# Attention with two feed-forwards: the second output product as seven products, and a new opening

## The chip, the core and the metric

The kernel runs on one core of one Trainium2 chip. The metric is the device time of one execution in microseconds. Before the change the median of three runs was 813.78 us (812.83 to 814.72). Every time below comes from these runs or from one profiled execution.

## The reference

Attention over 4 batches, 8 heads, 576 positions and 64 numbers a head (heads 0 to 3 see the last 32 positions, heads 4 to 7 every 32nd), then a gated feed-forward, then a second one whose hidden layer is the largest of three products. All tensors are float32.

```python
scores = np.where(masks, scale * np.matmul(q, k.transpose(0, 1, 3, 2)), -1e9)
attn = softmax(scores)                                # heads 0-3 local, 4-7 strided
x = np.matmul(attn, v).transpose(0, 2, 1, 3).reshape(2304, 512)
g = x @ w_gate                                        # 512 x 1536
x = (g * sigmoid(g) * (x @ w_val)) @ w_out            # 1536 x 512
h = np.maximum(np.maximum(x @ w1, x @ w2), x @ w3)    # 512 x 768 each
return h @ w_out2                                     # 768 x 512
```

## The kernel before

**Precision.** Every factor of a matmul is held as a high part in fp32r (a shorter float) and a low part, the difference. A product is three matmuls: high by high, high by low, low by high (`product`, `split`).

**First stage.** The rows of x are handled in five chunks of 512 or 448 tokens. Attention runs in blocks of two rows of 32 tokens for all heads; what it yields is split and kept as `xh`, `xl`. For each chunk and each of 12 blocks f of the hidden layer, the gate product (`ps_g`), the value product (`ps_v`) and the output product (`ps_y`) follow one another. In chunk 0 the raw 64-bit weights are loaded and rounded to float32 as well (`raw`; steps `size`, `rounding`, `sign`, `clamp`, `shift`, `rounded`), split, and stored for the later chunks.

The opening and chunk 0 run in the order of a table, `FIRST`, in which a letter is a step and a number the block or the weight: l and m load an attention block's queries, keys and values; S is its scores (L387), M, E, R the softmax, N its last step on POOL, T the transposes (L427), V their copy out of the banks, P the products with the values (L458), H and L the split into `xh` (L468) and `xl` (L474). r loads a raw weight, a, q, s, c, t, d round it, h and o split it, y stores it. G0 is the first half of the first gate product, b0 its second half, B and O are value and output products. The program order is the order of each engine's instructions there. `ON_SCALAR` lists the weights whose sign is taken on ScalarE (L209), with a cheaper shift on VectorE (L223); for the others POOL takes it (L211), with the dearer shift L225. All DMAs here are issued by SyncE, in program order.

**Between.** Chunks 1 to 4 are ordered by a scheduler. Steps named `later` convert the second stage's weights beside them: `pair_steps` makes, for w1, w2, w3 and each of three groups g of two blocks of h, the seven pieces of a Strassen-like product (seven half-size products in place of eight), `wo2_steps` splits the output weight of one block.

**Second stage.** Three passes p of 768 tokens, in two halves of 384 columns. In a pass there are nine `Group`s, g = 0 to 2 and i = 0 to 2 for w1 to w3. A group has `head`, `middle` and `tail` with 42 matmuls of 128x384 (L775): weight pieces (A11, A12, S3, A22, S1, S2, S4) come from a ring of four tiles of 1792 KB (`load_w`), the factors of y (B11, B21, T2, T1, T3, T4, B22) are made by sums and split once per pass (`load_y`, `split_y`, L173 and L176). A group's tail comes behind the next one's head. Copies of a bank to SBUF (`snap`, L789) and sums lead to four blocks of h; the last i takes the maximum, and its result is split per block. Then the output product follows: for each of six blocks j of 128 tokens, six blocks f of h stand in TensorE as weights and `wo2` (3072 KB, loaded once) streams through, 512 columns a time, 108 matmuls per pass (L849, banks `ps_z`). The first two j begin before the last tail with blocks f 0 to 3 (`z_early`). The y of the next pass is loaded during the first groups of this one.

## Time and profile before

| | us |
|---|---|
| median of three runs | 813.78 (812.83 to 814.72) |
| the profiled execution | 814.75 |
| its span | 813.0 |
| TensorE busy | 795.3 (98% of the span) |
| TensorE loading weights | 711.5 (88%) |
| VectorE busy | 542.8 (67%) |
| ScalarE busy | 384.2 (47%) |
| POOL busy | 235.6 (29%) |

The mean granted clock is 0.996. Busy times of matmuls overlap, since they are pipelined, so that 98% says that TensorE is seldom idle and not that it runs at its peak. The first stage ends near 530 us and the second begins there. In a row of a line or a tile, an arrow reads from right to left: the output's name stands left, the inputs' names right, and x counts instructions.

### The profile page before, as it was taken

The page shows a single profiled execution, that of the slowest core. Times are in us where ns is not written, and L with a number is a line of the kernel's source. Part 1 is how long each engine was busy: PE and PEld are TensorE (multiplying, and loading weights), DVE is VectorE, ACT ScalarE, POOL GpSimd, SP SyncE. Part 2 cuts the span into 40 slices and gives each one's busy share as a digit, 9 for nine tenths or more (in the row PEclk, how much of TensorE's full clock was granted, in tenths as well). Part 3 has the DMA queues.
Part 4 walks back from the last instruction along what each step waited for, and adds up shares of the span by engine and source line. Part 5 has one row for each costly group of instructions (what it writes and reads, how often), then busy time and mean ns, then how long its engine had stood idle before and what let it go on. Part 6 is the DMA issues. An engine that isn't in the chain of part 4 may idle for free.

```text
span 813.0 us, 12942 instructions
## 1 busy us (share of the span) xinstructions
PE 795.3 (98%) x4588; PEld 711.5 (88%) x4588; DVE 542.8 (67%) x1104; ACT 384.2 (47%) x856; POOL 235.6 (29%) x237
## 2 busy tenths in 40 slices
PE   6999999999999999999999999999999999999998
PEld 5777777888998998888999999999999989989986
DVE  5899997888969899799993863634454344613440
ACT  6999994455454634555342543423242123512220
POOL 2534442022312432314232664502212121402110
PEclk9899999999999999999999999999999999999999
DMA  9998887777766887757676997789646566634402
GB/s 281 322 326 290 303 311 270 262 242 226 261 235 208 264 285 246 264 208 258 231 262 212 346 392 294 281 342 354 237 181 232 168 210 213 260 148 181 181 1 77
DMA packets 69688, 200.50 MB, mean 247 GB/s; under 512 B 8088, under 2 KB 33432, under 8 KB 66040
## 3 DMA queue, kind: packets, MB, share of 16 engines
q1 hardware_dynamic: 69480, 199.55, 70.0%
q8 instruction: 36, 0.59, 0.3%
q14 instruction: 28, 0.23, 0.1%
q10 hardware_dynamic: 144, 0.13, 0.0%
HBM read 157.97 MB, written 41.68 MB: 246 GB/s over the span
## 4 chain that ended last, share of the span: by engine, by line
PE 55%; DVE 4%; DMA 2%; issue 1%; ACT 1%; SPq 0%; POOL 0%; DVEq 0%; ACTq 0%
PE ps_a L775 13%; PE ps_z L849 9%; PE ps_c L775 7%; PE ps_b L775 3%; PE ps_y L645 3%; PE ps_y L647 3%; PE ps_y L646 3%; PE ps_v L645 3%; PE ps_v L647 3%; PE ps_v L646 2%; PE ps_g L645 2%; PE ps_g L646 2%; PE ps_g L647 2%; DMA wr<-wsdr 1%; DVE pr L552 1%
## 5 line engine op out<-in xcount | busy, mean ns | idle before, releaser
L680 POOL TENSOR_TENSOR hl<-ht,hh 128x448 fp32r<-128x448 f32 x48 | 61.6, 1284 | 228.1 <-ACT hh L676 206.4
L176 POOL TENSOR_TENSOR hl<-t,hh 128x384 fp32r<-128x384 f32 x36 | 37.7, 1050 | 208.0 <-ACT hh L173 160.0
L775 PE MATMUL ps_a<-yhT,wr 128*128 128x384 f32 x324 | 94.6, 339 | 1.1 <-ACT s L789 1.1
L645 PE MATMUL ps_g<-xh,wh_g 128*128 128x448 f32 (+1 forms) x240 | 90.8, 378 | 1.0 <-ACT ht L664 1.0
L645 PE MATMUL ps_v<-xh,w_v 128*128 128x448 f32 (+1 forms) x240 | 91.2, 380 | 0.4 <-DVE ht L671 0.2
L646 PE MATMUL ps_g<-xl,wh_g 128*128 128x448 f32 (+1 forms) x240 | 89.8, 374 | 0.0
L647 PE MATMUL ps_y<-hh,w_o 128*128 128x448 f32 (+1 forms) x240 | 89.4, 373 | 0.3 <-DVE w_o L249 0.3
L647 PE MATMUL ps_g<-xh,wl_g 128*128 128x448 f32 (+1 forms) x240 | 89.5, 373 | 0.0
L646 PE MATMUL ps_y<-hl,w_o 128*128 128x448 f32 (+1 forms) x240 | 89.2, 372 | 0.0
L646 PE MATMUL ps_v<-xl,w_v 128*128 128x448 f32 (+1 forms) x240 | 89.2, 372 | 0.0
L647 PE MATMUL ps_v<-xh,w_v 128*128 128x448 f32 (+1 forms) x240 | 89.1, 371 | 0.0
L789 ACT ACTIVATE s<-ps_a 128x384 f32<-128x384 f32 x81 | 39.4, 490 | 99.0 <-PE ps_a L775 98.7
L676 ACT ACTIVATE hh<-ht 128x448 fp32r<-128x448 f32 (+1 forms) x60 | 35.3, 588 | 104.7 <-DVE ht L671 93.4
L645 PE MATMUL ps_y<-hh,w_o 128*128 128x448 f32 (+1 forms) x240 | 84.3, 380 | 0.0
L849 PE MATMUL ps_z<-wo2t,hh 128*128 128x512 f32 x216 | 64.8, 392 | 0.9 <-ACT osb L867 0.7
L775 PEld LDWEIGHTS ps_a<-yhT,wr 128*128 128x128 f32 x324 | 59.7, 188 | 2.6 <-ACT s L789 2.1
L775 PE MATMUL ps_a<-ylT,wr 128*128 128x384 f32 x162 | 54.8, 338 | 0.0
L645 PEld LDWEIGHTS ps_g<-xh,wh_g 128*128 128x128 f32 x240 | 45.4, 189 | 7.1 <-ACT ht L664 1.8
L645 PEld LDWEIGHTS ps_v<-xh,w_v 128*128 128x128 f32 x240 | 45.1, 188 | 6.5 <-DVE ht L671 1.1
L647 PEld LDWEIGHTS ps_g<-xh,wl_g 128*128 128x128 f32 x240 | 45.3, 189 | 5.4 <-DVE wl_g L249 0.4
L647 PEld LDWEIGHTS ps_y<-hh,w_o 128*128 128x128 f32 x240 | 45.1, 188 | 5.6 <-DVE w_o L249 0.7
L645 PEld LDWEIGHTS ps_y<-hh,w_o 128*128 128x128 f32 x240 | 45.0, 188 | 5.6
(150 smaller groups left out, 1843.2 us busy)
## 6 DMA issues: line engine op xcount, KB each, us to landing
wr<-wsdr SPq DMA_DIRECT2D x27, 1792.0 KB, 7.3
raw<-in_w_dram SPq DMA_DIRECT2D x60, 512.0 KB, 6.0
w_v<-wvdr SPq DMA_DIRECT2D x48, 512.0 KB, 4.5
w_o<-wodr SPq DMA_DIRECT2D x48, 512.0 KB, 4.6
wsdr<-whi SPq DMA_DIRECT2D x27, 256.0 KB, 2.9
wvdr<-w_v SPq DMA_DIRECT2D x12, 512.0 KB, 3.7
wodr<-w_o SPq DMA_DIRECT2D x12, 512.0 KB, 3.9
wsdr<-w SPq DMA_DIRECT2D x18, 256.0 KB, 3.3
```

The source lines that it names most:

```text
L176: return a.ins, lo_eng.tensor_tensor(lo, src, f32(hi), ALU.subtract).ins
L552: eng.tensor_tensor(pv, self.k[:, 0:i + 1, :], self.q[:, r:r + 1, :].to_broadcast([128, i + 1, D]), ALU.mult)
L645: nc.tensor.matmul(ps, wh, xh, start=first, stop=False)
L646: nc.tensor.matmul(ps, wh, xl, start=False, stop=False)
L647: nc.tensor.matmul(ps, wl, xh, start=False, stop=last)
L676: return nc.scalar.activation(hs[c, f][0], t, AF.Copy).ins
L680: return eng.tensor_tensor(hl, t, f32(hh), ALU.subtract).ins
L775: nc.tensor.matmul(ps, wts[:, c, a, ks], y[k][b], start=first and k == q == 0, stop=k == 1 and q == 2, skip_group_check=True,)
L789: nc.scalar.activation(s, self.a, AF.Copy)
L849: nc.tensor.matmul(z[j], a[:, ts], w[:, f, b], start=f == q == 0, stop=f == NF2 - 1 and q == 2)
```

## The change

The output product of the second feed-forward takes the seven-product form too, and it is turned: pieces of w_out stand as weights, h streams with 384 columns, and the output is stored transposed (the host turns it). `pair_steps` makes the pieces of w_out (i = 3) in place of `wo2_steps`, and they come through the ring, which has five tiles now: 36 loads of 1792 KB, where there were 27 and one of 3072. A pass has 126 matmuls of 128x384 for it (`Out`, `outputs`), the parts with g = 0 and 1 of three pieces before and behind the last group's tail. h is no longer split per block; its seven factors are made and split per group (`Factors`). What is to be converted waits in a list (`waiting`), from which `some(n)` takes entries at chosen places. The y of the next pass is loaded at the end of a pass, into single buffers. The second stage and the last two blocks of the last chunk run in program order, without the scheduler.

The table `FIRST` is new: the first raw weight's load stands behind the sixth block's (l5, m5), the transposes, copies and products of the blocks stand in another order, and so do the steps of chunk 0. Five more weights take their sign on ScalarE, the copies of blocks 3, 6 and 7 and the high part of block 3 go to VectorE.

```diff
@@ -53,34 +53,34 @@
-l0 k0 l1 l2 l3 l4 m4 k1 r0 l5 m5 l6 m6 l7 m7 r1 r2 r3 r4 S0 M0 S1 E0 M1 S2 E1 R0 M2 S3 N0 T0 E2 M3 S4 R1
...
+l0 k0 l1 l2 l3 l4 m4 k1 l5 m5 r0 l6 m6 l7 m7 r1 r2 r3 r4 S0 M0 S1 E0 M1 S2 R0 E1 N0 M2 S3 E2 R1 T0 M3 N1
+S4 V0 E3 R2 T1 P0 N2 M4 V1 T2 R3 P1 E4 V2 N3 H0 S5 L0 T3 H1 M5 P2 V3 E5 L1 P3 R4 N4 H3 a0 S6 R5 q0 c0 L3
...
-ON_SCALAR = range(5, 3 * NF, 2)
-
-NRING = 4
+ON_SCALAR = (0, 3, 4, 5, 7, 9, 10, 11, 13, 15, 17, 18, 19, 21, 23, 25, 27, 29, 31, 33, 35)
+
+NRING = 5
...
+    OUT_PIECES = ("A11", "S3", "A12", "A22", "S1", "S2", "S4")
...
+            if i == 3:
+                a12, a21 = a21, a12
...
-    def wo2_steps(f):
...
+        eng = nc.vector if (c, f) == (NC - 1, NF - 1) else nc.gpsimd
+        last_val[:] = [m, high_h(c, f, t), low_h(c, f, t, eng)]
...
+    class Factors:
...
+        def combine(self):
+            b12 = self.raw["T3"]
+            nc.vector.tensor_tensor(self.fresh("T1"), b12, self.raw["B11"], ALU.subtract)
+            nc.gpsimd.tensor_tensor(b12, self.raw["B22"], b12, ALU.subtract)
+            nc.vector.tensor_tensor(self.fresh("T2"), self.raw["B22"], self.raw["T1"], ALU.subtract)
+            nc.vector.tensor_tensor(self.fresh("T4"), self.raw["B21"], self.raw["T2"], ALU.subtract)
+
+        def split(self, f):
+            src = self.raw.pop(f)
+            hi, lo = self.part("h", f), self.parts.get(f) or self.part("l", f)
+            self.parts[f] = hi, lo
+            split(hi, lo, src, nc.scalar, nc.gpsimd if f in ("T3", "B22") else nc.vector)
+
+    waiting = []
+
+    def some(n):
+        for _ in range(min(n, len(waiting))):
+            waiting.pop(0)()
+
+    def conversion(fs, names):
+        return [fs.combine] + [lambda f=f: fs.split(f) for f in names]
+
+    def load_y(p):
+        y = [Factors(y_p, f"y{k}") for k in range(2)]
...
+        for k in range(2):
+            waiting.extend(conversion(y[k], FACTORS[:-1]))
+        waiting.extend(lambda k=k: y[k].split("B22") for k in range(2))
...
+            t = to = run[blk]
+            if self.i == 2:
+                h2.setdefault(self.g, Factors(h2_p, f"h{self.g}"))
+                to = h2[self.g].fresh("T3") if blk == "12" else t
+                h2[self.g].raw.setdefault("B" + blk, t)
             if s is None:
-                nc.vector.tensor_tensor(t, ps, t, ALU.max)
+                nc.vector.tensor_tensor(to, ps, t, ALU.max)
             else:
                 nc.vector.tensor_tensor(s, ps, s, ALU.add)
-                nc.vector.tensor_tensor(t, s, t, ALU.max)
-            if self.i == 2:
-                f, h = 2 * self.g + int(blk[0]) - 1, int(blk[1]) - 1
-                hh, hl = h2[f]
-                ts = slice(h * TB, (h + 1) * TB)
-                split(hh[:, ts], hl[:, ts], t, nc.scalar, nc.gpsimd)
+                nc.vector.tensor_tensor(to, s, t, ALU.max)
 
...
+        def finish(self):
+            if self.i == 2:
+                waiting.extend(conversion(h2[self.g], FACTORS))
...
-    def mm(j, fs):
-        if True:
-            if j not in z:
-                z[j] = z_p.tile([128, 512], F32, name="ps_z", tag="z")
-            ts = slice(j * 128, (j + 1) * 128)
-            for f in fs:
-                (hh, hl), w = h2[f], wo2
-                for q, (a, b) in enumerate(((hh, 0), (hh, 1), (hl, 0))):
-                    nc.tensor.matmul(
-                        z[j], a[:, ts], w[:, f, b], start=f == q == 0, stop=f == NF2 - 1 and q == 2
-                    )
-
-    def out2(p):
...
+    class Out:
...
+        def mul(self, n, piece, f, gs=range(NFP), last=False):
+            ms = slice(self.m * 128, (self.m + 1) * 128)
+            factor_product(
+                getattr(self, n), OUT_PIECES, piece, [(self.w[g], ms) for g in gs], [h2[g].parts[f] for g in gs],
+                gs[0] == 0 and piece in ("A11", "A12", "S1"), last
+            )
+
...
+        def emit(self, blk, ps, s=None):
+            t0 = (2 * PASSES[self.p] + int(blk[1]) - 1) * TB
+            rows = slice((int(blk[0]) - 1) * 256 + self.m * 128, (int(blk[0]) - 1) * 256 + (self.m + 1) * 128)
+            osb = osb_p.tile([128, TB], F32, name="osb", tag="osb")
+            if s is None:
+                nc.scalar.activation(osb, ps, AF.Copy)
             else:
-                nc.scalar.activation(osb, z[j], AF.Copy)
-            nc.sync.dma_start(out[t0:t0 + 128, :], osb)
-
-        for j in range(2 * TB // 128):
-            mm(j, z_late if j < 2 else range(NF2))
-            done(j)
-        z.clear()
-
+                nc.vector.tensor_tensor(osb, ps, s, ALU.add)
+            nc.sync.dma_start(out[rows, t0:t0 + TB], osb)
+
+    def outputs(p, grp, y):
+        early = range(NFP - 1)
+        final = [NFP - 1]
+        o = [Out(p, m) for m in range(2)]
+        o[0].mul("a", "A11", "B11", early)
+        grp.tail()
+        o[0].mul("b", "A12", "B21", early)
+        o[0].mul("c", "S1", "T1", early)
+        o[1].mul("a", "A11", "B11", early)
+        o[1].mul("b", "A12", "B21", early)
+        o[1].mul("c", "S1", "T1", early)
+        grp.finish()
+        ends = p == NP - 1
+        some(len(waiting))
+        if not ends:
+            y = load_y(p + 1)
+            load_w(*work[len(ring)])
+        for t in o:
+            t.mul("a", "A11", "B11", final)
+            t.snap(1)
+            t.mul("b", "A12", "B21", final, True)
+            t.emit("11", t.b, t.s1)
+        some(4)
+        for t in o:
+            t.mul("a", "S2", "T2")
+            t.snap(2)
+            some(1)
+        for t in o:
+            t.mul("c", "S1", "T1", final)
+            t.mul("a", "S3", "T3")
+            t.snap(3)
+            t.emit("22", t.c, t.s3)
+            some(2)
+        for t in o:
+            some(2)
+            if ends and t is o[1]:
+                t.mul("c", "S4", "B22", last=True)
+                t.emit("12", t.c, t.s2)
+                t.mul("a", "A22", "T4", last=True)
+                t.emit("21", t.a)
+            else:
+                t.mul("a", "A22", "T4", last=True)
+                t.emit("21", t.a)
+                t.mul("c", "S4", "B22", last=True)
+                t.emit("12", t.c, t.s2)
+        for _ in range(NFP):
+            if len(ring) < len(work):
+                load_w(*work[len(ring)])
+        return y
...
-            return nc.vector if i in (0, 2, 5) else nc.scalar
+            return nc.vector if i in (0, 2, 3, 5, 6, 7) else nc.scalar
...
-            "H": lambda i: blocks[i].high(nc.vector if i in (0,) else nc.scalar),
+            "H": lambda i: blocks[i].high(nc.vector if i in (0, 3) else nc.scalar),
...
-        later += [step for f in range(NF2) for step in wo2_steps(f)]
+        later += [step for g in range(NFP) for step in pair_steps(3, g)]
...
+            if (c, f) == (NC - 1, SEAM + 1):
+                seam.enter_context(tc.manual_schedule())
...
+                for n in range(SEAM + 1, NF):
+                    reload("v", n)
+                    reload("o", n)
+                y = load_y(0)
...
+            if c == NC - 1:
+                some(len(waiting) if f == NF - 1 else 5)
...
+        for p in range(NP):
+            work += [(p, g, i) for g in range(NFP) for i in range(3)] + [(p, g, 3) for g in range(NFP)]
         for n in range(1, NRING):
-            last = load_w(*work[n])
-        with tc.issue_after(last):
-            nc.sync.dma_start(f32(wo2), wo2dr)
+            load_w(*work[n])
+        ctx.enter_context(tc.manual_schedule())
         before = None
-        for n, (p, g, i) in enumerate(work):
-            if (g, i) == (0, 0):
-                for f in range(NF2):
-                    h2[f] = tuple(h2_p.tile([128, 2 * TB], F32R, name=f"h{q}{f}", tag=f"h{q}{f}") for q in "hl")
-            if (g, i) == (0, 2) and p + 1 < NP:
-                with tc.issue_after(last):
-                    raw = [load_y(p + 1, k) for k in range(2)]
-            grp = Group(p, g, i, y)
-            grp.head()
-            if before is not None:
-                before.tail()
-            grp.middle()
-            before = grp
-            if n + NRING < len(work):
-                last = load_w(*work[n + NRING])
-            if (g, i) == (NFP - 1, 2):
-                mm(0, z_early)
-                grp.tail()
-                mm(1, z_early)
-                before = None
-                out2(p)
-                if p + 1 < NP:
-                    y = [split_y(raw[k]) for k in range(2)]
-
+        for p in range(NP):
+            h2.clear()
+            for g in range(NFP):
+                for i in range(3):
+                    grp = Group(p, g, i, y)
+                    grp.head()
+                    some(2)
+                    if before is not None:
+                        before.tail()
+                    grp.middle()
+                    if before is not None:
+                        before.finish()
+                    some(4)
+                    if before is not None:
+                        if len(ring) < len(work):
+                            load_w(*work[len(ring)])
+                    before = grp
+            y = outputs(p, grp, y)
+            before = None
```

On TensorE around the last block's scores, before: `L387` is scores (`qke` and `loct` are queries and keys of two rows), `L427` transposes, `L458` products with values, `L645` to `L647` the first gate product. For `L387` and `L458` the trace counts two instructions where these rows count one.

```order
L387 MATMUL ps_a<-qke 64x96 x8
L458 MATMUL ps_a<-raw 64x64 x16
L387 MATMUL ps_a<-qke 64x96 x8
L427 MATMUL ps_a<-cst,qke 96x128 x16
L645 MATMUL ps_g<-xh,wh_g_407 128x512
L646 MATMUL ps_g<-xl,wh_g_407 128x512
L647 MATMUL ps_g<-xh,wl_g_408 128x512
```

The second row of scores is block 7's; the transposes of blocks 4 to 7 follow it together. Further on, around the end of the first half of the gate product:

```order
L647 MATMUL ps_g<-xh,wl_g_408 128x512
L458 MATMUL ps_a<-qke,ve 64x64 x32
L387 MATMUL ps_a<-loct 64x96 x16
L645 MATMUL ps_g<-xh,wh_g_407 128x512
L646 MATMUL ps_g<-xl,wh_g_407 128x512
```

The products of blocks 4 to 7 and the scores of blocks 8 and 9 stand between the two halves. On TensorE after, around block 7's scores (`L376`, `L416`, `L447`, `L634` to `L636` are the same operations):

```order
L447 MATMUL ps_a<-raw 64x64 x16
L376 MATMUL ps_a<-qke 64x96 x8
L416 MATMUL ps_a<-cst,qke 96x128 x8
L376 MATMUL ps_a<-qke 64x96 x8
L447 MATMUL ps_a<-qke,ve 64x64 x16
L634 MATMUL ps_g<-xh,wh_g_428 128x512
L635 MATMUL ps_g<-xl,wh_g_428 128x512
```

The transposes of blocks 4 and 5 moved ahead of these scores, their products right behind them. And around the end of the first half of the gate product:

```order
L636 MATMUL ps_g<-xh,wl_g_429 128x512
L416 MATMUL ps_a<-cst,qke 96x128 x8
L447 MATMUL ps_a<-qke,ve 64x64 x16
L376 MATMUL ps_a<-loct 64x96 x8
L634 MATMUL ps_g<-xh,wh_g_428 128x512
L635 MATMUL ps_g<-xl,wh_g_428 128x512
```

Between the halves there are now the transposes and products of blocks 6 and 7 and the scores of block 8 alone.

On SyncE at the opening, before (`raw<-in_w_dram` is a raw weight, `qke` and `ve` are an attention block's queries, keys and values):

```order
L186 DMA raw<-in_w_dram 128x1024
L371 DMA qke<-in_locqk_dram 128x640
L375 DMA ve<-in_locv_dram 96x512
L371 DMA qke<-in_locqk_dram 128x640
L375 DMA ve<-in_locv_dram 96x512
L371 DMA qke<-in_locqk_dram 128x640
L375 DMA ve<-in_locv_dram 96x512
L186 DMA raw<-in_w_dram 128x1024 x5
```

The first raw weight stands ahead of the last three blocks. On SyncE at the same place after:

```order
L360 DMA qke<-in_locqk_dram 128x640
L364 DMA ve<-in_locv_dram 96x512
L186 DMA raw<-in_w_dram 128x1024
L360 DMA qke<-in_locqk_dram 128x640
L364 DMA ve<-in_locv_dram 96x512
L360 DMA qke<-in_locqk_dram 128x640
L364 DMA ve<-in_locv_dram 96x512
L186 DMA raw<-in_w_dram 128x1024 x4
```

It moved behind one more attention block, the sixth, and the other raw weights stay behind the eighth.

On ScalarE at the end of the first pass, after: `L801` copies a bank to SBUF, `L173` makes a high part (`h2h` of the last group's h, `y0h` of the next pass's y), `L884` copies a finished output.

```order
L801 ACTIVATE s_6581<-ps_a 128x384
L173 ACTIVATE h2hB_6652<-t_6387 128x384
L173 ACTIVATE h2hB_6656<-t_6483 128x384
L173 ACTIVATE h2hT_6660<-rT_6648 128x384
L173 ACTIVATE h2hT_6664<-rT_6645 128x384
L173 ACTIVATE h2hT_6668<-rT_6612 128x384
L173 ACTIVATE h2hT_6672<-rT_6650 128x384
L173 ACTIVATE h2hB_6676<-t_6427 128x384
L801 ACTIVATE s_6701<-ps_a 128x384
L801 ACTIVATE s_6712<-ps_a 128x384
L173 ACTIVATE y0hB_6727<-y0lB_6680 128x384
L173 ACTIVATE y0hB_6730<-y0lB_6686 128x384
```

The seven splits of the last group's h stand in one row, and those of the next y begin between the output product's copies. On ScalarE near the same place before, with `L789` the same copy:

```order
L789 ACTIVATE s_6514<-ps_a 128x384
L173 ACTIVATE yhT_6723<-rT_6088 128x384
L789 ACTIVATE s_6764<-ps_a 128x384
L173 ACTIVATE yhT_6703<-rB_6066 128x384
L789 ACTIVATE s_6528<-ps_a 128x384
L173 ACTIVATE yhT_6731<-rB_6081 128x384
L789 ACTIVATE s_6780<-ps_a 128x384
L173 ACTIVATE hh_5956<-t_6407 128x384
L173 ACTIVATE yhT_6707<-rT_6074 128x384
```

The splits of the next y stood ahead of the pass end, among the last groups' own copies, and h was split block by block; y's splits moved behind the last group.

## Rows read from the trace of the kernel before

**Rows 1.** Table by stretches: length, busy PE, PEld, DVE, ACT, POOL, PEclk, DMA

```profile
20.00:30.00 10.00, 7.97 (x86) 6.88 (x86) 6.22 (x24) 8.40 (x25) 6.29 (x8) 0.66 1.04 361
30.00:110.00 80.00, 78.58 (x534) 61.40 (x531) 79.21 (x191) 76.18 (x181) 31.49 (x39) 1.00 0.88 308
...
440.00:530.00 90.00, 90.00 (x446) 83.40 (x445) 50.90 (x72) 40.50 (x79) 48.60 (x43) 1.00 0.88 316
530.00:813.00 283.00, 276.57 (x1462) 260.06 (x1460) 115.04 (x196) 80.49 (x166) 50.96 (x48) 1.00 0.54 198
```

**Rows 2.** Chain of waits in the second stage: start, us, what

```profile
552.02 2.12 PE ps_a L775 x12
...
628.55 4.12 PE ps_z L849 x18
```

**Rows 3.** The same table for lines L775 and L849 alone: PE, PEld

```profile
530.00:813.00 283.00, 206.96 (x1134) 200.05 (x1134) 1.00 0.54 198
...
530.00:813.00 283.00, 81.30 (x324) 60.19 (x324) 1.00 0.54 198
```

**Rows 4.** Tiles of both lines: ns min/median/max, first and last start in us

```profile
L775 PEld LDWEIGHTS ps_a<-yhB,wr x108: 186/188/188, 530.7 to 779.6; 128*128 128x128 f32 x108
...
L849 PE MATMUL ps_z<-wo2t,hl x108: 387/389/501, 554.9 to 809.0; 128*128 128x512 f32 x108
```

**Rows 5.** TensorE's waits in 530 to 813: us in total, times, longest

```profile
PE ps_a L775 <- ACT s L789: 1.1, 2, 0.6
PE ps_z L849 <- ACT osb L867: 0.7, 1, 0.7
PE ps_b L775 <- DMA wr<-wsdr: 0.7, 1, 0.7
```

**Rows 6.** Table by stretches, first part of the second stage (last column GB/s)

```profile
520.00:560.00 40.00, 40.00 (x217) 38.45 (x216) 13.19 (x25) 12.12 (x24) 6.42 (x6) 1.00 0.95 373
```

**Rows 7.** Splits by line, 560 to 813: busy us, mean ns, idle before

```profile
L173 ACT ACTIVATE hh<-t 128x384 fp32r<-128x384 f32 x33 | 17.3, 524 | 36.4 <-DVE t L809 25.4 <-DVE t L806 10.7
...
L176 DVE TENSOR_TENSOR ylT<-rB,yhT 128x384 fp32r<-128x384 f32 x4 | 2.2, 554 | 3.2 <-ACT yhT L173 3.2
...
L176 POOL TENSOR_TENSOR hl<-t,hh 128x384 fp32r<-128x384 f32 x35 | 36.7, 1051 | 185.3 <-ACT hh L173 137.3 <-issue 21.5 <-PE ps_a L775 19.3
```

**Rows 8.** DMA issues, 530 to 813: count, KB each, us to landing

```profile
wr<-wsdr SPq DMA_DIRECT2D x23, 1792.0 KB, 7.2
...
rB<-ydr SPq DMA_DIRECT2D x12, 192.0 KB, 7.7
```

**Rows 9.** TensorE in time at the opening: start, us, instruction, idle before

```profile
18.61 0.88 PE L387 MATMUL ps_a<-qke 64*64 64x96 f32 x16 [0.40 <-DMA qke<-in_locqk_dram]
22.03 3.62 PE L427 MATMUL ps_a<-cst,qke 128*96 128x128 f32 x16 [2.54 <-DVE xl L474]
...
28.08 2.09 PE L458 MATMUL ps_a<-qke,ve 96*64 96x64 f32 x64
...
31.82 0.49 PE L645 MATMUL ps_g<-xh,wh_g 128*128 128x512 f32 x1
```

**Rows 10.** POOL in time at the opening; then a DMA issue of 0 to 40

```profile
23.02 0.83 POOL L415 TENSOR_TENSOR qke<-qke,state 128x384 f32<-128x384 f32 x1 [0.75 <-ACT xh L468]
...
raw<-in_w_dram SPq DMA_DIRECT2D x13, 512.0 KB, 9.6
```

**Rows 11.** Operations of chunk 0 by line, 0 to 152: busy us, mean ns

```profile
L225 DVE SCALAR_TENSOR_TENSOR w<-w,raw 128x512 int32<-128x512 int32 x20 | 16.5, 835 | 1.6 <-POOL w L217 1.6
L209 ACT ACTIVATE q<-raw,mh 128x512 f16<-128x512 int32 x16 | 14.0, 878 | 0.0
L223 DVE TENSOR_SCALAR w<-w 128x512 int32<-128x512 int32 x16 | 9.3, 578 | 0.0
...
L432 ACT ACTIVATE qke<-ps_a 96x512 f32<-96x512 f32 x3 | 1.7, 591 | 0.7 <-PE ps_a L427 0.6
L434 DVE COPY qke<-ps_a 96x512 f32<-96x512 f32 x1 | 0.7, 687 | 0.8 <-PE ps_a L427 0.8
```

More of the change, by code (lines that the diff above doesn't have):

```diff
@@ L437, in pv @@
             self.outputs()
[L438 removed]
+            self.high()
             self.low()
@@ new lines, in tile_attention_swiglu_maxout @@
+    waiting = []
[7 more added lines that the diff above has]
+        for k in range(2):
+            for n in ("B11", "B12", "B22", "B21"):
+                if n == "B12":
+                    r = y[k].fresh("T3")
+                else:
+                    y[k].parts[n] = y[k].part("l", n)
+                    r = y[k].raw[n] = f32(y[k].parts[n])
+                m, t = 2 * int(n[1]) - 2 + k, (2 * PASSES[p] + int(n[2]) - 1) * TB
+                for c, i0, i1, o in pieces(t // STRIDE, (t + TB) // STRIDE):
+                    nc.sync.dma_start(
+                        r[:, o * STRIDE:(o + i1 - i0) * STRIDE], ydr[c][:, m, i0 * STRIDE:i1 * STRIDE]
+                    )
+        for k in range(2):
+            waiting.extend(conversion(y[k], FACTORS[:-1]))
+        waiting.extend(lambda k=k: y[k].split("B22") for k in range(2))
@@ L985, in tile_attention_swiglu_maxout @@
         s2_p = sub(two, "s2", 2, reuse_waits="tile")
[L986 to L987 removed]
+        osb_p = sub(two, "osb", 4, reuse_waits="tile")
         h2_p = sub(two, "h2", 1, reuse_waits="tile")
[L989 removed]
         m_p = sub(two, "m", 2, space=PS, reuse_waits="tile")
[L991 to L992 removed]
@@ L1026 @@
 ]
-_OUTS = [((NT, DM), "float32")]
+_OUTS = [((DM, NT), "float32")]
 def kernel(**inputs):
```

176 lines of the change are left out of this document (69 added, 107 removed).

## The prediction

> **What bounds the kernel now.** I read the table by stretches first, then the chain of waits inside the last stretch, then what TensorE waits for there. In the table TensorE is full from 440 to 530, idles 1.4 us in the 80 from 30 to 110, and 6.4 in the 283 of the second feed-forward [rows 1]. So a change pays where it takes columns off TensorE or fills a gap, and work on the other engines costs only where they keep TensorE waiting. The stretch 30 to 110 is the one to watch for that: VectorE is busy 79.21 of 80 us there and ScalarE 76.18 [rows 1].
>
> In the second feed-forward the chain is TensorE nearly throughout, and it shows what one matmul costs in a run: 2.12 us for 12 of 384 columns, 176.7 ns each, and 4.12 us for 18 of 512 columns, 228.9 ns each [rows 2]. The busy time of single matmuls (389 ns for the one with 512 columns) is of no use for this, since they overlap [rows 4].
>
> The stage runs from 530.7 to the start of its last matmul at 809.0, 278.3 us, or 278.5 with that one's interval [rows 4]. It holds 1134 matmuls of the seven products and 324 of the output product [rows 3]: 1134 x 0.1767 + 324 x 0.2289 = 200.4 + 74.2 = 274.6, so that about 3.9 us are stalls. TensorE's waits give 1.1 us behind ScalarE copies, 0.7 behind one of the output's copies and 0.7 behind a ring load, 2.5 in all [rows 5]; the rest is refilling, and weight loads that wait for the last group's split h.
>
> **Output product.** Per pass, 108 matmuls of 512 columns become 126 of 384 (2 halves of m, 7 pieces, 3 groups, 3 matmuls each for the hi and lo parts). 108 x 0.2289 = 24.7 against 126 x 0.1767 = 22.3, so -2.46 a pass and **-7.4** for three. In the order of the changed kernel 1512 matmuls of 384 columns stand in this stage and none of 512, so the kernel does what it says.
>
> A weight load takes 188 ns, more than the 176.7 ns between two matmuls [rows 2, 4]; in 520 to 560 the load row is busy 38.45 of 40 us, and the matmuls still follow at 176.7 [rows 2, 6]. So loads and columns overlap, and the columns set the pace. The Trainium skill ("Perfetto Trace Analysis", Identifying the Most-Contended Engine) says that matmul busy time misleads and that headroom on TensorE is judged by how busy the weight loads are. By that rule the change spends the scarce thing, since it adds 54 loads; the second rival below is what this would give. Intervals shorter than a load speak against it in this trace.
>
> **Stalls of the stage.** The pass end is written anew. In the old one the output product waits for the last group's h to be split. In the new one early output products with groups 0 and 1 (2 halves of m, 3 pieces, 2 groups, 3 matmuls: 36) and the 12 of the last group's tail, 48 x 0.1767 = 8.5 us, lie between that group's middle and the first use of its h. Its conversion is three VectorE sums, one POOL sum and seven splits, each a copy of 0.52 us on ScalarE and a difference of 0.55 on VectorE or 1.05 on POOL [rows 7]. The first two pieces need one split each, and the later ones are wanted 2 to 4 us apart: I see cover for h. The y of the next pass is now loaded at the pass end, where it was loaded most of a pass ahead: 8 transfers, which took 7.7 us to land [rows 8], then two sets of sums and 14 splits, while 15 us of output products are left. ScalarE gets 14 x 0.52 = 7.3 us of splits there, and 10 copies of like length: 12.5 of 15. Tight, but it fits. I put the stalls at 1.5 us in all, nearer to the low end, since each of these chains has cover by its rows: **-2.4**. The bounds are 0.5 (every cover holds) and 8 (each of the three pass ends loses over 2), or -3.4 and +4.1.
>
> The ring now carries 36 loads of 1792 KB instead of 27 and one of 3072. A pass moves 12 x 1.835 MB, 1.57 of y and 1.57 of output, 25.2 MB in 504 x 0.1767 = 89.1 us, or 283 GB/s. The stretch 520 to 560 moved 373 GB/s [rows 6], so I cost it at nothing; the third rival is its price if that cover is gone.
>
> **Opening.** On TensorE half of the transposes, copies and products of blocks 4 to 7 move ahead of block 7's scores or right behind them, and block 9's scores move behind the first gate product. Before: block 7's scores start at 18.61 and take 0.88; TensorE idles 2.54 us; transposes from 22.03 for 3.62; six gate matmuls; 64 small products from 28.08 for 2.09; the scores of blocks 8 and 9; the rest of the gate product from 31.82 [rows 9]. The granted clock is 0.66 on the mean of 20 to 30 [rows 1], so a part of these ten microseconds, behind the idle time, ran at the lower of the two levels, 1.2 GHz. With the new order, what must follow block 7's scores is its exponentials and POOL's step, which ended at 23.02 + 0.83 = 23.85 [rows 10], half the transposes (1.8 at most), a copy of 0.6 to 0.7 [rows 11], half the products (1.0) and block 8's scores (0.9): 23.85 + 1.8 + 0.7 + 1.0 = 27.3, with block 8's scores beside block 7's last split. So at best -4.5 at the start of that product, and -3.6 once block 9's 0.9 us, only moved, are paid.
>
> Against it stands the load of chunk 0. Five more signs go from POOL to ScalarE: 5 x 0.878, less three copies of 0.59 and one split that go to VectorE, near +2.2. VectorE: 3 x 0.69 and that split, less 5 x (0.835 - 0.578) for cheaper shifts, near +1.2 [rows 11]. These engines are nearly full in 30 to 110 [rows 1], but so is TensorE; I let 1.4 us of it show. That makes **-2.2**. Bounds: -4.5 (the best start, and block 9's scores find a gap) and +2 (no gain, and ScalarE's load shows whole). The first raw weight now stands behind the sixth block on SyncE's queue; it took 9.6 us to land [rows 10], and a microsecond of delay would stay inside these bounds.
>
> **The rest.** From 150 to 440 the order of TensorE is unchanged: 0. In 440 to 530 the preparation of w_out has seven pieces instead of four, near 8 us more on VectorE and 3 on ScalarE by the splits' price, where they are busy 50.90 and 40.50 of 90 us beside a full TensorE [rows 1]: 0, and +1 if a split comes between. At the end one copy and one transfer stand for two of each: 0 within 0.3.
>
> **Sum.** -7.4 - 2.4 - 2.2 = -12.0. The profiled execution took 814.75 us with a span of 813.0, 1 us over the median of 813.78; taken off its own time that gives 802.7, and **801.8** for the median. All good ends together: -7.4 - 3.4 - 4.5 = -15.3, 798.5. All bad ends: -7.4 + 4.1 + 2 + 1 = -0.3, 813.5.
>
> **Rivals.** First, ScalarE and VectorE take back the opening's gain in chunk 0. Their 76.18 and 79.21 of 80 us speak for it, TensorE's 78.58 against. Then -7.4 - 2.4 = -9.8: 804.0, chance 0.18. Second, weight loads set the pace of the output product: 378 x 0.188 = 71.1 against 74.2 us, -3.1 in place of -7.4: 806.1. Matmuls 176.7 ns apart speak against it; 0.04. Third, on the other side, the ring: if its loads land only one after the other, 1.835 MB in 7.2 us or 255 GB/s [rows 8], a pass takes 25.2 / 0.255 = 98.8 us instead of 89.1, and the second and third pass lose 9.7 us each: 821. It makes the kernel slower from 265 GB/s down, where a pass takes 95 us and two times 6 us eat the gain. The 373 GB/s of 520 to 560 speak against it; 0.05. Fourth, order on the other engines: they take instructions as written, so a split of y that waits for its transfer holds the copies queued behind it on ScalarE, which free TensorE's banks. With y landing 3 us late at two pass ends, 6 us: 807.8. That y is now loaded late speaks for it, the ring's 5 tiles do not help; 0.09. My own case has 0.62, and 0.02 is left for what I don't see.
>
> **How the numbers follow.** The likeliest is my own case, 801.8, which spreads from 798 to 805. The rivals at 804, 806 and 807.8 belong to the range, the one at 821 does not: 797.5 to 808.0, with some 0.12 outside on both sides. About 0.2%, 1.6 us, is what a measurement of this kernel can tell from no change. Faster by more than that are all cases but the third rival and part of the unseen: 0.92. The same needs most bad ends at once, or the third rival mildly: 0.03. Slower: 0.05.
>
> **What would show it.** In the trace of the changed kernel: runs of the output product's matmuls at 176 to 177 ns; some 269 us from the second stage's first matmul to its last; TensorE's waits there under 2 us in all; the rest of the first gate product beginning 3 to 4 us before 31.82, and chunk 1 only some 2 us earlier. Wrong would be: waits on ring loads in passes two and three, splits of y or h as releasers for more than a microsecond each, intervals near 188 ns in the output product, or a granted clock below 1 behind a stall.

## The result and the profile after

The changed kernel takes 799.82 us in the median (five runs, 797.38 to 801.72) against 813.78 (five runs, 811.62 to 814.72): a ratio of 0.9832 with an interval of 0.9807 to 0.9856, 14.0 us less. Forecast were 801.8 us, a range of 797.5 to 808.0 and a chance of 0.92 for faster. The profiled execution of the changed kernel took 797.38 us, its span is 795.6, and so it is the fastest of its five; that of before was 1 us above its median. The two traces differ by 17.4 us, 3.4 more than the medians do, and one question of the experiments is where these lie.

The page's busy times and chain of the changed kernel (us, share of the span, instructions):

```profile
span 795.6 us, 13312 instructions
PE 782.2 (98%) x4642; PEld 713.5 (90%) x4642; DVE 613.4 (77%) x1206; ACT 400.6 (50%) x903; POOL 231.1 (29%) x225
...
PE 88%; DVE 5%; ACT 4%; DMA 1%; issue 1%; POOL 1%; SPq 0%; DVEq 0%
```

VectorE works 70 us more than before and TensorE 13 less; TensorE holds 88% of the chain. The table by stretches, for [rows 1] (length, busy PE, PEld, DVE, ACT, POOL, granted clock, DMA share, GB/s):

```profile
10.00:20.00 10.00, 8.25 (x136) 5.95 (x132) 9.37 (x50) 9.33 (x43) 3.49 (x5) 0.83 1.04 314
20.00:30.00 10.00, 9.33 (x109) 6.79 (x106) 8.93 (x25) 9.55 (x25) 7.67 (x9) 1.00 1.04 362
30.00:110.00 80.00, 78.58 (x504) 61.66 (x504) 78.20 (x184) 77.24 (x175) 28.32 (x36) 1.00 0.89 314
...
440.00:530.00 90.00, 90.00 (x448) 83.33 (x447) 68.46 (x91) 43.53 (x87) 48.78 (x44) 1.00 0.99 358
530.00:795.00 265.00, 262.12 (x1492) 261.76 (x1490) 169.15 (x274) 92.45 (x204) 49.03 (x39) 1.00 0.68 254
```

In 440 to 530 VectorE has 17.6 us more work, where I had put near 8, and TensorE is still full: the pieces of w_out cost nothing there. In 30 to 110 TensorE is as full as before.

At the last pass end the chain of waits of the kernel before ran through VectorE and ScalarE, which summed and copied the last group's h and an output while TensorE waited (start, us, what):

```profile
789.89 0.57 DVE s L808
...
790.49 1.15 DVE t L809
...
792.09 0.58 ACT osb L867
...
792.72 16.64 PE ps_z L849 x72
```

At the first pass end of the changed kernel:

```profile
595.09 1.04 PE ps_c L790 x6
596.13 1.06 PE ps_a L790 x6
...
601.40 3.17 PE ps_a L790 x18
604.57 0.53 PE ps_c L790 x3
```

TensorE alone, 3.17 us for 18 matmuls, 176 ns each. The view of TensorE's waits from 520 us on is empty for this kernel, where it had three rows before [rows 5]. From the last matmul of the first stage (start 526.92) to the last of all (791.79) there are 264.87 us for 1506 matmuls, 175.9 ns apiece, since six of the 1512 run before. Before, the same measure is 278.62 us: 1134 x 0.1759 + 324 x 0.2289 = 273.6, with 5.0 us of stalls. So 378 matmuls in 66.5 us take the place of 324 in 74.2, and all 5.0 us of stalls are gone: 12.7 us in all.

The opening on TensorE, for [rows 9]:

```profile
19.14 0.96 PE L376 MATMUL ps_a<-qke 64*64 64x96 f32 x16
20.22 1.23 PE L447 MATMUL ps_a<-qke,ve 96*64 96x64 f32 x32
...
22.91 0.60 PE L416 MATMUL ps_a<-cst,qke 128*96 128x128 f32 x4
23.77 0.64 PE L416 MATMUL ps_a<-cst,qke 128*96 128x128 f32 x4 [0.26 <-POOL qke L404]
...
26.68 0.50 PE L634 MATMUL ps_g<-xh,wh_g 128*128 128x512 f32 x1
```

The gap of 2.54 us behind block 7's scores is filled with products, the second half of the gate product begins at 26.68 instead of 31.82, and chunk 1 (here and below, its first value product) at 144.29 instead of 148.90. That is 4.6 us, twice what I had put. With the 12.7 of the second stage and 0.2 at the end it makes up the 17.4 of the two traces, so the 3.4 us that the medians do not have lie ahead of chunk 1.

### The profile page after: what moved, and what is told of

Same layout as the page of the kernel before. It is cut to its first block, busy times and chain, and to the rows that moved or that the text cites. A ratio compares the mean times of both kernels' runs of the same rounds, so it can differ in the third digit from the quotient of the medians.

```text
span 795.6 us, 13312 instructions
## 1 busy us (share of the span) xinstructions
PE 782.2 (98%) x4642; PEld 713.5 (90%) x4642; DVE 613.4 (77%) x1206; ACT 400.6 (50%) x903; POOL 231.1 (29%) x225
## 4 chain that ended last, share of the span: by engine, by line
PE 88%; DVE 5%; ACT 4%; DMA 1%; issue 1%; POOL 1%; SPq 0%; DVEq 0%
PE ps_a L790 19%; PE ps_c L790 10%; PE ps_v L634 6%; PE ps_y L634 6%; PE ps_y L635 6%; PE ps_y L636 6%; PE ps_g L634 6%; PE ps_v L636 5%; PE ps_v L635 5%; PE ps_g L635 5%; PE ps_g L636 5%; PE ps_b L790 5%; PE ps_a L376 2%; PE ps_a L447 1%; PE ps_a L416 1%
## 5 line engine op out<-in xcount | busy, mean ns | idle before, releaser
L801 ACT ACTIVATE s<-ps_a 128x384 f32<-128x384 f32 x99 | 48.4, 489 | 135.2 <-PE ps_a L790 135.2
L634 PE MATMUL ps_g<-xh,wh_g 128*128 128x448 f32 (+1 forms) x240 | 90.6, 377 | 2.1 <-DVE ht L693 1.1
L634 PE MATMUL ps_v<-xh,w_v 128*128 128x448 f32 (+1 forms) x240 | 91.1, 380 | 0.2 <-DVE ht L660 0.2
L636 PE MATMUL ps_y<-hh,w_o 128*128 128x448 f32 (+1 forms) x240 | 89.3, 372 | 0.0
L636 PE MATMUL ps_v<-xh,w_v 128*128 128x448 f32 (+1 forms) x240 | 89.3, 372 | 0.1
L636 PE MATMUL ps_g<-xh,wl_g 128*128 128x448 f32 (+1 forms) x240 | 89.1, 371 | 0.0
L634 PE MATMUL ps_y<-hh,w_o 128*128 128x448 f32 (+1 forms) x240 | 83.9, 379 | 0.0
L740 POOL TENSOR_TENSOR rT<-t,rT 128x384 f32<-128x384 f32 x9 | 12.5, 1390 | 149.6 <-DVE rT L739 149.6
L790 PE MATMUL ps_a<-y0hT,wr 128*128 128x384 f32 x162 | 54.9, 339 | 0.0
L790 PE MATMUL ps_a<-y1hT,wr 128*128 128x384 f32 x162 | 54.5, 337 | 0.0
L634 PEld LDWEIGHTS ps_g<-xh,wh_g 128*128 128x128 f32 x240 | 45.1, 188 | 8.5 <-ACT ht L653 1.8
L634 PEld LDWEIGHTS ps_v<-xh,w_v 128*128 128x128 f32 x240 | 45.1, 188 | 6.3 <-DVE ht L660 0.8
L636 PEld LDWEIGHTS ps_v<-xh,w_v 128*128 128x128 f32 x240 | 45.1, 188 | 5.4 <-DVE w_v L249 0.5
L634 PEld LDWEIGHTS ps_y<-hh,w_o 128*128 128x128 f32 x240 | 45.0, 188 | 5.4
L635 PEld LDWEIGHTS ps_g<-xl,wh_g 128*128 128x128 f32 x240 | 45.1, 188 | 5.1 <-DVE xl L463 0.4
L636 PEld LDWEIGHTS ps_y<-hh,w_o 128*128 128x128 f32 x240 | 45.1, 188 | 5.1 <-DVE w_o L249 0.3
L636 PEld LDWEIGHTS ps_g<-xh,wl_g 128*128 128x128 f32 x240 | 45.1, 188 | 5.0 <-DVE wl_g L249 0.2
```

Source lines behind the costliest of these rows:

```text
L634: nc.tensor.matmul(ps, wh, xh, start=first, stop=False)
L635: nc.tensor.matmul(ps, wh, xl, start=False, stop=False)
L636: nc.tensor.matmul(ps, wl, xh, start=False, stop=last)
L740: nc.gpsimd.tensor_tensor(b12, self.raw["B22"], b12, ALU.subtract)
L790: nc.tensor.matmul(ps, w[:, c, a, ks], b, start=first and n == q == 0, stop=last and n == len(wts) - 1 and q == 2, skip_group_check=True,)
L801: nc.scalar.activation(s, ps, AF.Copy)
```

## Experiments

Times are medians. Unless the text says otherwise, each is compared with the changed kernel's 799.82 us. The runs were made in three rounds; the kernel before took 813.77, 812.69 and 812.71 us in them, so that a difference of 1 us between rounds tells nothing.

**The changed kernel again.** No edit.

> The changed kernel itself, once more, for a second trace of it. Both theories expect a median near 799.8 us. If the gain of the second stage is fixed (its matmuls follow at 175.8 ns with no wait) and the executions differ in the opening, the second stage's last matmul lies again 264.9 us behind the first stage's last, within 0.3, and what differs from the first trace stands already at the first matmuls of chunk 1. If the second stage varies from run to run, its length differs by one or more microseconds.

Measured: 800.83 us, 798.24 to 802.17. The second stage takes 264.89 us, as in the first trace to 0.02. The second half of the gate product begins at 30.79, not 26.68, and chunk 1 at 147.14, not 144.29. Its opening on TensorE:

```profile
20.23 0.64 PE L416 MATMUL ps_a<-cst,qke 128*96 128x128 f32 x4 [0.96 <-POOL qke L404]
20.80 1.15 PE L376 MATMUL ps_a<-qke 64*64 64x96 f32 x16
22.30 1.98 PE L447 MATMUL ps_a<-qke,ve 96*64 96x64 f32 x32 [0.35 <-DVE qke L423]
...
25.66 0.63 PE L634 MATMUL ps_g<-xh,wh_g 128*128 128x512 f32 x1
26.08 0.63 PE L635 MATMUL ps_g<-xl,wh_g 128*128 128x512 f32 x1
```

The order is the same. Here TensorE waits for POOL and VectorE near 20 us, and then its clock is at the lower level, 1.2 GHz (a granted clock of 0.50 from 22 to 27): the first gate matmuls start 0.43 us apart, where 0.23 is usual. In the first trace the lower level came in 10 to 20 (a granted clock of 0.83) and was over when the gate product began. So one execution tells little of an opening. In the ten traces of this study that run the new order, with all its loads in the new places and all signs on ScalarE as listed, the second half begins between 26.68 and 32.08, 28.9 in the median, and chunk 1 between 144.29 and 148.39, 146.4 in the median; the two of the old order have 31.82 and 32.30, and 148.90 and 149.44.

**The old opening in the changed kernel.**

```diff
-FIRST, ON_SCALAR, evictor and "H" of the changed kernel
+FIRST, ON_SCALAR, evictor and "H" of the kernel before
```

> The changed kernel with the table of the opening, the list of signs on ScalarE and the copies' engines of before. Theory 1 (the opening's order gives the 4.6 us that stand between the two traces at the start of chunk 1): 4.6 us above the changed kernel, near 804.4, and the second half of the first gate product near 31.8 us. Theory 2 (the medians: 14.0 less 12.6 of the second stage, so that the opening gives 1.4 and the trace of after was an early one): 801.2, ratio to before 0.985. Theory 3 (chunk 0's ScalarE and VectorE take all of it back): 799.8.

Measured: 801.57 us, 799.5 to 804.6: 1.7 more, near theory 2. These executions overlap with the changed kernel's (797.38 to 801.72), so that this pair alone does not tell theory 2 from theory 3. Its trace also has the longer of two intervals in the last chunk (last section), 1.7 us that do not come from the opening.

**The new opening in the kernel before.** The same edit the other way.

> The kernel before with the new table, signs and copies alone; the second stage stays as it was. Theory 1: 813.8 - 4.6 = 809.2. Theory 2: 812.4. Theory 3: 813.8. In all of them the second stage keeps its 278.6 us from the first stage's last matmul to its own last.

Measured: 811.44 us against 813.77 in the same round, a ratio of 0.9969 (0.9955 to 0.9984), which is 1.3 to 3.7 us less; the second stage keeps 278.0. Between theories 1 and 2. Both traces of this pair have the shorter interval in the last chunk, so that this is the firmer figure. By times the opening is worth some 2 us, by the traces' median at chunk 1 (146.4 against 149.2) 2.7; my -2.2 stands, and the trace's 4.6 was a lucky execution.

**The old signs.**

```diff
-ON_SCALAR = (0, 3, 4, 5, 7, 9, 10, 11, 13, 15, 17, 18, 19, 21, 23, ..., 35)
+ON_SCALAR = range(5, 3 * NF, 2)
```

> The changed kernel with the sign of the five weights (0, 3, 4, 10, 18) back on POOL and the dearer shift on VectorE, in the new order. If the load of ScalarE in chunk 0 is what takes back part of the gain, it is faster by up to 2 us: 798. If ScalarE was not the limit, it is the same, or slower because POOL's sign (0.82 us) and the dearer shift (0.84 for 0.58) of the first gate weight stand in the chain of the first gate product: up to 1 us later at that product's start, 800 to 801.

One weight's sign comes behind its shift in this order, so that its values are not the reference's; the work is. Measured: 802.89 us, 799.69 to 804.35, slower by some 3 us and not faster; up to 1.7 of these can be the longer interval in the last chunk, which its trace has too. Chunk 1 begins at 148.53, later than in all ten traces above. So taking these signs off ScalarE gains nothing. VectorE's share of the first rival is not tested here, since the dearer shifts give it more work.

**No early parts.**

```diff
-        early = range(NFP - 1)
-        final = [NFP - 1]
+        final = range(NFP)
...
-        (the six products with early around the tail)
```

> The changed kernel without the early parts: the 36 matmuls with groups 0 and 1 that stood around the last tail of a pass follow with the rest, so that only the 12 of the tail and 6 more stand between the last group's middle and the first use of its h. Theory (the early parts are the cover that took the stalls away): the low part of B11 is ready some 1 to 2 us after TensorE wants it, at each of three pass ends, with its restart: +3 to +6 us over the changed kernel. Rival (the order of the splits alone took the stalls away, and the early parts are not needed): within 1 us.

Measured: 817.31 us, 17.5 more than the changed kernel and slower than the one before (ratio 1.0048, 1.0028 to 1.0068). In the trace the second stage takes 278.74 us, 13.9 more. TensorE's waits there, and the chain at the first pass end:

```profile
PE ps_a L790 <- DVE h2lB L176: 8.8, 3, 2.9
PE ps_a L790 <- ACT s L801: 1.7, 3, 0.6
```

```profile
596.34 0.57 DVE s L832
...
596.93 0.57 DVE rT L833
...
597.52 0.57 DVE rT L739
...
598.12 0.57 DVE rT L741
...
598.71 1.23 DVE rT L742
599.94 0.48 DVE h2lB L176
```

The low part of B11 stands in VectorE's order behind all sums of the conversion, though it needs none of them, and the third sum takes 1.23 us instead of 0.56. So it comes 4.1 us behind the tail. That is the chain that the early parts cover. With the slower matmul behind each, the two waits cost 4.1 us a pass end, 12.2 in all; 1.5 more is the lower clock behind the long wait of the first pass end (below). The theory holds, and it had the price too low: I had thought of a wait of 1 to 2 us, and it is 2.9. The median of 17.5 is 3.6 above what this trace shows, whose execution took 813.84 us; where these lie no trace here tells.

**Half of the early parts.**

```diff
-        early = range(NFP - 1)
-        final = [NFP - 1]
+        early = range(1)
+        final = range(1, NFP)
```

> The changed kernel with the early parts of group 0 alone: 18 matmuls per pass instead of 36 lie around the last tail, the other 18 follow with the last group's. From the run without early parts: B11's low part is ready 4.1 us behind the tail's end. Here 15 + 3 matmuls lie between, 3.2 us, so TensorE should wait 0.9 to 1.0 us at each of three pass ends, and some 0.1 ahead of the tail (0.53 us of early work against a wait of 0.58): in all +3.3 to +3.6 us for the second stage, 268.3 us from the first stage's last matmul on. If the wait came from something other than this chain, it stays near 0 or near the 3 us of the run without early parts.

Measured: 805.70 us, and 270.03 us for the second stage, +5.2. The waits are those expected:

```profile
PE ps_a L790 <- DVE h2lB L176: 2.7, 3, 0.9
```

0.9 us at each pass end: the chain of 4.1 us less 3.2 of cover. Refilling behind them and waits near the tail and before the next piece that are too short for the view bring the rest of the 5.2, where I expected 3.3 to 3.6. From 36 matmuls over 18 to none, the wait goes from 0 over 0.9 to 2.9. In the changed kernel 30 matmuls behind the tail, 5.3 us, are the cover, and in its trace the low part is ready 1.1 us before TensorE's first use of it, at each of the three pass ends.

**The next y later.**

```diff
-            y = load_y(p + 1)
             load_w(*work[len(ring)])
+            y = load_y(p + 1)
```

> The changed kernel with the ring load of 1792 KB issued ahead of the next pass's y instead of behind it, at two pass ends; y lands some 4 to 5 us later. In the trace of the changed kernel VectorE has no idle time from 601.6 to 615.2, and what it does there is mostly y's sums and splits. Theory (VectorE's row of work has no slack, and rival four of the prediction had the right price): two times 3 to 4 us, +6 to +8. Rival (y lands with several microseconds to spare): within 1 us.

Measured: 801.88 us; the second stage takes 265.68 us, 0.8 more, with one wait of 0.5. My expectation was wrong and the rival right. VectorE at the first pass end, in the changed kernel and then here (this trace lies 6.05 us later from the first stage on):

```profile
601.61 1.01 DVE L886 TENSOR_TENSOR osb<-ps_b,s 128x384 f32<-128x384 f32 x2
602.54 0.54 DVE L739 TENSOR_TENSOR rT<-rT,y0lB 128x384 f32<-128x384 f32 x1
```

```profile
607.66 1.01 DVE L886 TENSOR_TENSOR osb<-ps_b,s 128x384 f32<-128x384 f32 x2
608.59 0.54 DVE L739 TENSOR_TENSOR rT<-rT,y0lB 128x384 f32<-128x384 f32 x1
```

Both times y's first sum follows at once behind the same output sum: VectorE comes to it only then. In the changed kernel the inputs of this sum had landed at 595.90, 6.6 us ahead of it; here they landed at 608.20, 0.4 us ahead. So y had been waiting for VectorE and not VectorE for y. At the second pass end the slack was used up: the inputs of the next sums came late, ScalarE waited for one, the bank copy queued behind that split was late, and TensorE waited for the copy.

```profile
698.85 0.53 ACT L173 ACTIVATE y0hB<-y0lB 128x384 fp32r<-128x384 f32 x1 [1.84 <-DMA y0lB<-ydr]
...
700.21 0.44 PE L790 MATMUL ps_a<-h0hT,wr 128*128 128x384 f32 x1 [0.53 <-ACT s L801]
```

That is the mechanism of the prediction's fourth rival, at 0.8 us: it needs y some 6 us later than in the changed kernel to begin. An engine that is busy without a gap says nothing on how late its inputs may be.

**Four ring tiles.**

```diff
-NRING = 5
+NRING = 4
```

> The changed kernel with a ring of four tiles, as before. Loads took 8.2 us to land in the trace of the changed kernel and a group takes 7.4 us, so that four tiles still give some 20 us ahead. If the ring's loads had been near their limit (rival three), waits on ring loads appear, a few microseconds each at the pass ends, where four tiles are asked for at once; if not, the second stage keeps its 264.9 us within 0.5. I expect 1 to 3 us of waits, at the pass ends alone.

Measured: 809.65 us, 9.8 more, and 275.41 us for the second stage. The wait, and the chain that leads to it:

```profile
PE ps_a L790 <- DMA wr<-wsdr: 6.6, 2, 3.5
```

```profile
617.39 0.48 DVE osb L886
...
617.89 0.36 SPq L887
...
618.30 0.02 SPq L783
...
618.35 7.52 DMA wr<-wsdr
...
625.91 2.29 PE ps_a L790 x6
```

The load took 7.5 us, which is its usual time [rows 8]. It was late because it was issued late, and two things delay the issue. A pass takes 12 loads, so with four tiles this load goes to the tile that holds the first pieces of w_out, and the output product reads them to its end; their last matmul:

```profile
615.84 0.33 PE L790 MATMUL ps_c<-h0hB,wr 128*128 128x384 f32 x1
```

From there to the issue at 618.35 some 2 us more go by, since SyncE issues in order, and the pass's last output stores, which wait for VectorE's last sums, stand ahead of the load. An estimate from these rows: issued at 616.2, the load would have landed at 623.7, and TensorE, which wanted it at 622.4, would have waited 1.3 us instead of 3.5. So the larger part of this wait is the queue's, and the rest is the missing tile. With five tiles the same load has a tile that is free behind the last group's tail, and it is issued at 596.41, ahead of the output product. My expectation of some 20 us ahead overlooked that w_out holds three of the four tiles until the pass ends. Waits of 6.6 us and a lower clock behind them make up the 10.5.

**The first raw weight ahead again.**

```diff
-l0 k0 l1 l2 l3 l4 m4 k1 l5 m5 r0 l6 m6 ...
+l0 k0 l1 l2 l3 l4 m4 k1 r0 l5 m5 l6 m6 ...
```

> The changed kernel with the first raw weight's load back ahead of the sixth block's. My step: the sixth block's keys land up to 1.7 us later and the weight 1 to 2 us earlier; since the first gate product waits for the blocks' chain and not for the weight, the start of its second half is later by 0 to 1 us: 800 to 801 us. If the weight is what it waits for, it is earlier by up to 1 us.

Measured: 801.21 us, 799.22 to 801.52. In its trace the gate product's second half begins at 31.77, which lies inside the spread of the new order (26.68 to 32.08), near its late end. The time points to some 1 us later and the trace to a late start, and neither can tell it from none.

**Eight pieces.**

```diff
         o[0].mul("c", "S1", "T1", early)
+        o[0].mul("c", "S1", "T1", early)
         o[1].mul("a", "A11", "B11", early)
+        o[1].mul("a", "A11", "B11", early)
...
         o[1].mul("c", "S1", "T1", early)
+        o[1].mul("c", "S1", "T1", early)
```

> The changed kernel with 18 matmuls more per pass, three early products made twice (the second overwrites the first): as many as an output product of eight pieces would have. Theory (TensorE's columns set the pace, 175.8 ns each): 54 x 0.1758 = 9.5 us more, so that one product of eight is worth 9.5 us and the turn from 512 to 384 columns costs 2.1 of them. Rival (the pass end hangs on VectorE, which is full there, and more time on TensorE gives it room): 3 to 6 us more.

Measured: 808.57 us, and the second stage takes 274.23 us, +9.36 for the 9.5 expected. So the output product is priced by its matmuls' columns: seven products instead of eight save 9.4 us. With eight it would take 66.5 + 9.4 = 75.9 us at 384 columns, where 512 columns took 74.2; so the turn to narrower columns by itself costs 1.7.

**Half the columns.**

```diff
-                    ps, w[:, c, a, ks], b, start=first and n == q == 0,
+                    ps[:, cut], w[:, c, a, ks], b[:, cut], start=first and n == q == 0,
...
+                cuts = (slice(0, TB // 2), slice(TB // 2, TB)) if pieces is OUT_PIECES else (slice(0, TB),)
```

> The changed kernel with every matmul of the output product cut into two of 192 columns: the same columns, 378 more matmuls and weight loads. Theory (columns set the pace, at 384 / 175.8 ns or one column per 0.417 ns and some 16 ns each): 96 ns each, 756 x 0.096 = 72.6 against 66.5 us, +6. Rival (a weight load holds TensorE for its 188 ns, as the rule on load time would have it): 756 x 0.188 = 142 us, +76. Between them, a load has a price of its own below 188 that 384 columns hide, and the interval shows it.

Each half starts its own sum in a bank that the other half is using, so the output product's values are not the reference's; the work is all there. Measured: 820.08 us, 20.3 more, and the second stage takes 283.20 us, 18.3 more. The chain of waits at a pass end:

```profile
601.36 1.34 PE ps_a L792 x12
602.70 1.34 PE ps_b L792 x12
```

111.7 ns for 192 columns. That is neither the 96 of the columns nor the 188 of a load's row. So a load keeps TensorE for 112 ns at most and not for the 188 that its row shows, and at 384 columns, 176 ns, it hides. That the load is what sets the 112 ns is likely, but no run shows it.

**A split end.**

```diff
+            nc.scalar.activation(a[:, :h], ps[:, :h], AF.Copy)
+            nc.vector.tensor_copy(b[:, :h], ps[:, h:])
+            nc.scalar.dma_start(out[rows, t0:t0 + h], a[:, :h])
+            nc.sync.dma_start(out[rows, t0 + h:t0 + TB], b[:, :h])
```

> The changed kernel with the last output tile copied in two halves of 192 columns, one on ScalarE and one on VectorE at the same time, each stored by a queue of its own. Both theories agree on the size: the copy takes 0.3 instead of 0.49 us and each transfer half the bytes, so the span behind the last matmul falls from 3.8 us by 0.2 to 0.4. That is below what the times can tell, and is read from the trace. If the end hangs on the transfer's fixed time alone, it stays within 0.1.

Measured: 798.97 us. From the last matmul's start to the end there are 3.82 us, against 3.81: nothing gained.

```profile
793.66 0.33 ACT L894 ACTIVATE osb<-ps_a 128x192 f32<-128x192 f32 x1 [4.28 <-PE ps_a L790]
794.02 0.38 ACTq L896 DMA_DIRECT2D out_dram<-osb  x1
794.02 0.36 DVE L895 COPY osb<-ps_a 128x192 f32<-128x192 f32 x1 [1.40 <-ACT osb L894]
```

VectorE waits for ScalarE's copy of the other half, so that the two copies take 0.72 us together, where one took 0.49. In the trace VectorE's copy waits for the semaphore that ScalarE's copy sets, so the program as built made it wait; what two copies at the same time would bring was not tested. No version beat the changed kernel beyond the spread of its runs.

## Why the prediction was right

**Output product.** Right in mechanism and size: -7.4 forecast, 74.2 - 66.5 = 7.7 measured. That the columns and not the loads set the pace was the reading of 176.7 ns between matmuls beside loads of 188 [rows 2, 4]; the eighth product (+9.4 us) shows it again, and the rival of loads at 188 is excluded by the halves at 112.

**Stalls.** Right in direction, too small: -2.4 forecast, 5.0 before and none after, beyond even my bound of -3.4. Two things were off. The stalls of before were 5.0 and not 3.9, since I took 176.7 ns for 384 columns from a short run where the long one gives 175.9: 1134 x 0.8 ns is 0.9 us. And I kept 1.5 us of new stalls for a pass end that has none. The cover for h was named and is shown by the runs with half and without the early parts. But I gave the first two pieces one split each and counted 8.5 us of cover; the low part of the first piece is ready only 4.1 us behind the tail, since its split is queued behind the sums, and the cover from there is 5.3. That was enough, with 1.1 to spare, so the step came out right with a margin thinner than I thought.

**y at the pass end.** I called ScalarE tight, 12.5 of 15 us. VectorE is the one that is full there, without idle time from 601.6 to 615.0. The fourth rival, y landing late, did not come about in the changed kernel, where y lands some 6 us ahead; the run with the late y used that up, and then its mechanism cost 0.8 us.

**Ring.** "I cost it at nothing" was right for five tiles. The third rival named another mechanism, transfers one after the other. With four tiles 10 us are lost though the load takes its usual 7.5 us: no tile is free for it until the output product ends, and then it stands behind the output's stores on SyncE. I had read the ring's bytes and neither its tiles nor its queue; the prediction's step on SyncE should have gone through the pass end as well. The fifth tile is part of why the step came out right, and the prediction gives it no such part.

**Opening.** -2.2 forecast; 1.7 and 2.3 by times, 2.7 in the median of the traces. The first rival, chunk 0 taking the gain back, is excluded by the new opening in the kernel before, which is faster by 1.3 to 3.7 us with all of that load. In the traces' medians 3.2 us at the second half of the gate product (28.9 against 32.1) are still 2.7 at chunk 1, so that some 0.5 was taken back, where I had let 1.4 show. The place of the first raw weight is too small to tell.

**The rest.** I put 8 us more on VectorE in 440 to 530, and it is 17.6. TensorE is full there all the same, so the step's cost of nothing was right and its price was not.

**Sum.** -7.7 - 5.0 - 2.0 = -14.7 against the -14.0 of the medians. The difference is inside the spread of single executions, of which the last section shows a part. The forecast of -12.0 was 2.0 us short, and the second stage is where: -12.7 against the -9.8 that I had put.

## What to carry to other kernels

A product in fewer and narrower matmuls is priced by the interval in a long run of them, and its stalls by the chain that feeds the first matmul behind the switch; work that needs none of that chain belongs there, and removing half of it measures the slack. Read an in-order queue's position and when the target of a transfer is free, and not its bytes alone, before calling a transfer free. And an opening that hangs on the first transfers needs several traces: here one trace was off by 2 us, as much as the effect itself.

## What the runs showed of the hardware

**Two cadences.** In the last chunk the 448-column matmuls of the first stage follow at 202.7 ns on the mean in nine traces and at 206.7 in five, with the same code and order of these matmuls, at a granted clock of 1.00, for all of the 87 us: 1.7 us of difference. In the first they alternate (199 to 207 ns), in the second all are 206 or 207. Each of two traces of the changed kernel itself has the shorter one; the longer one is found with the old opening, with the old signs, without early parts, with the late y and with halves, whose edits have nothing to do with this stretch. Both are found on one and the same chip, the shorter with the changed kernel again and the longer with the old opening. What sets it stays open, and with it whether the comparisons of these five carry the 1.7 us in all their executions.

**The clock behind a wait.** With four ring tiles, TensorE waited 3.5 us at one pass end, and the matmuls behind it:

```profile
625.91 0.69 PE L790 MATMUL ps_a<-y0hB,wr 128*128 128x384 f32 x1 [3.48 <-DMA wr<-wsdr]
626.39 0.53 PE L790 MATMUL ps_a<-y0lB,wr 128*128 128x384 f32 x1
626.71 0.53 PE L790 MATMUL ps_a<-y0hB,wr 128*128 128x384 f32 x1
627.03 0.53 PE L790 MATMUL ps_a<-y1hB,wr 128*128 128x384 f32 x1
```

From the third on they start 320 ns apart, 17 of them in a row, where 176 is usual: 2.4 us on top of the wait. The granted clock there (the number behind POOL's) is 0.50, the lower level of 1.2 GHz:

```profile
626.00:632.00 6.00, 6.00 (x19) 6.00 (x20) 1.12 (x2) 0.49 (x1) 0.00 (x0) 0.50 1.02 437
```

After the other pass end's wait of 3.1 us ten were slow. Without early parts the first wait of 2.9 us was followed by ten slow ones, and the second and third, as long, by none. So a wait of 3.5 us at a pass end cost 1.7 times its length, and two of 2.9 us little more than themselves.
